# Sparse attention and a two-layer expert on one core: full-array attention matmuls over 64-query tiles, laid between the expert's matmuls by hand

## The chip, the core and the metric

The kernel runs on one core of one Trainium2 chip. A core has a matrix engine (TensorE, PE in the profile), a vector engine (VectorE, DVE), a scalar engine for activations (ScalarE, ACT), a general one (GpSimd, POOL), an engine that issues transfers (SyncE, SP), and 16 DMA engines that move data between HBM and the on-chip memory SBUF. TensorE reads its operands from SBUF and writes to a second on-chip memory, PSUM, from which VectorE and ScalarE read. Both memories have 128 partitions (rows).

The metric is device time in microseconds. The kernel before takes 463.11 us, the median of 3 runs (462.93 to 463.98).

## The reference

The inputs are `q`, `k`, `v` of 4 batches x 8 heads x 768 positions x 64, and the weights `moe_w_in` (512 x 2048) and `moe_w_out` (2048 x 512), all in float32. What matters of the computation:

```python
block, window = (32, 16);  nb = S // block          # 24 blocks of 32 keys
k_sum = k.reshape(B, H, nb, block, D).max(axis=3)   # one key per block: the maximum
v_sum = v.reshape(B, H, nb, block, D).mean(axis=3)  # one value per block: the mean
scores_l = scale * q @ k.T, kept only where |i - j| < window, else -1e9
scores_s = scale * q @ k_sum.T + log(block)
a = softmax(concatenate([scores_l, scores_s], axis=-1))
attn_out = a @ concatenate([v, v_sum])              # B, H, S, D
x = attn_out.transpose(0, 2, 1, 3).reshape(B * S, H * D)   # 3072 x 512
h = x @ w_in
out = (h / (1 + exp(-1.702 * h))) @ w_out           # 3072 x 512
```

A query thus sees at most 31 near keys, each with its own weight, and 24 block keys. Since `log(block)` is added to a block's score, its weight is 32 times `exp`, which with the block's mean is `exp` times the block's sum. The kernels use that: the block's value is the sum of its 32 values and its entry in the denominator is 32.

## The kernel before, in words

The kernel has three stages in a row. The framework places the waits and buffers and decides within each engine in which order instructions go out; it may move one ahead of another that isn't ready.

**Attention** (L121 to L216) is a loop over 4 batches and 8 heads. Per head, q and k come in as six row tiles of 128 positions side by side (`raw`, L124 and L127), ScalarE casts them to bf16 (`cb`, L131), and six TensorE transposes (L134) give q with the head dimension on partitions 0 to 63 and k on 64 to 127. VectorE copies this out of PSUM (`qkT`, L138), and a transfer moves the k half down to partitions 0 to 63 (`kTb`, L141), since both operands of a matmul lie on the same partitions. VectorE takes the maximum over each block of 32 keys (`ksumT`, L144). The values come in as eight windows of 128 keys, one per tile of 96 queries (`vwf`, L151 to L155), and are cast by ScalarE (`vwin`, L158) with a column of ones added, so that the value matmul also makes the denominator. Eight small matmuls against constant 0/1 matrices sum the values by block (`ps_vs`, L170).

Queries go in tiles of 96, four tiles to a group, two groups to a head. One matmul of 384 columns makes a group's scores against the 24 block keys (L179), four of 96 columns its scores against the window's 128 keys (L185). ScalarE exponentiates both (L190, L192), and VectorE multiplies the near part by a 0/1 mask (L194). Each query tile then has two value matmuls into the same output: one over 128 near keys (L200), one over 24 block keys (L203). VectorE divides by the denominator (L208, L210), and a transfer writes the group to a buffer in HBM, `x_bridge` (L213).

**Weights** (L230 to L239): two transfers of 4 MB each and two casts on ScalarE.

**The expert** (L241 to L270) is a loop over six chunks of 512 tokens. Four transposing transfers read `x_bridge` back (`xsb`, L244). Sixteen groups of four matmuls of 512 columns make `ph` (L252), and ScalarE applies the activation (`gT`, L257). Then four groups of sixteen matmuls make `po` (L262), which ScalarE copies out (`osb`, L268) and a transfer stores (L270).

All transfers go out on SP's queue. GpSimd only makes the constants at the start.

## Time and profile before

| | |
|---|---|
| median of 3 runs | 463.11 us (462.93 to 463.98) |
| span of the profiled execution, first to last instruction | 460.9 us |
| TensorE busy in the span | 370.1 us (80%), 2032 matmuls |
| ScalarE busy | 186.0 us (40%) |
| VectorE busy | 111.8 us (24%) |
| GpSimd busy | 6.9 us (1%) |
| bytes moved | 45.46 MB, 124064 of 131771 packets under 512 bytes |
| chain of work that ended last | PE 66%, DMA 14%, DVE 10%, ACT 5% |

The profile comes from one execution, and its span is 2.2 us below the median of the runs. In it a group of instructions is named by its line, engine, operation, output and input; behind the bar stand its busy time, the mean duration of one in ns, and the idle time of the engine before it with what ended that. PEld is TensorE's loading of a matmul's fixed operand, which overlaps its matmuls. Matmuls are pipelined, so the distance between two starts (the pitch) says more than the duration of one. PEclk is the clock granted to TensorE, as a share of full speed.

### The profile page before, as it was taken

Reading aid. Unit: us, or ns where it says so; the run is one execution under the profiler, and the core shown is the slowest. Engines: PE = TensorE matmul, PEld = TensorE weight load, DVE = VectorE, ACT = ScalarE, POOL = GpSimd, SP = SyncE. Lnnn points to the kernel's source line nnn. Section 1 sums busy time; section 2 is a strip of 40 time slices with the busy share of each in tenths; the row PEclk is TensorE's granted clock in tenths of the full one; section 3 lists DMA queues with packets and bytes.
Section 4 is the critical chain, followed back from the end, with each engine's and each line's share of the span. In section 5 each row is a group of like instructions: output and inputs, shape, how many; then the busy total and the mean of one; then the engine's idle time right before and its main releaser. Section 6 shows DMA issues by size and latency. Waiting matters only on the chain.

```text
span 460.9 us, 5530 instructions
## 1 busy us (share of the span) xinstructions
PE 370.1 (80%) x2032; PEld 206.4 (45%) x2048; DVE 111.8 (24%) x320; ACT 186.0 (40%) x316; POOL 6.9 (1%) x38
## 2 busy tenths in 40 slices
PE   3986777876967877777777703799999999999996
PEld 2554455554644544555454500344444444444442
DVE  1443534443444443444444400000000000000000
ACT  3443343433434343342443255643616345262541
POOL 5000000000000000000000000000000000000000
PEclk9999999999999999999999999899999999999999
DMA  7445544544455365364445699222040410101101
GB/s 156 87 100 112 111 97 96 108 102 105 98 120 115 78 139 110 80 133 90 105 106 111 213 387 249 46 36 102 7 109 23 75 64 1 73 18 47 46 24 69
DMA packets 131771, 45.46 MB, mean 99 GB/s; under 512 B 124064, under 2 KB 126112, under 8 KB 131232
## 3 DMA queue, kind: packets, MB, share of 16 engines
q1 hardware_dynamic: 131744, 45.11, 40.3%
q8 instruction: 16, 0.26, 0.2%
q14 instruction: 11, 0.09, 0.1%
HBM read 29.36 MB, written 9.44 MB: 84 GB/s over the span
## 4 chain that ended last, share of the span: by engine, by line
PE 66%; DMA 14%; DVE 10%; ACT 5%; issue 2%; SPq 2%; ACTq 0%
PE ph L252 18%; PE po L262 18%; PE ps_av L203 12%; PE ps_av L200 11%; DMA kTb<-qkT 9%; DVE ksumT L144 6%; PE ptp L134 4%; DMA w_out_f<-in_moe_w_out_dram 4%; PE ps_blk L179 3%; DVE qkT L138 2%; ACT w_out_sb L239 2%; DMA raw<-in_k_dram 1%; ACT cb L131 1%; DVE xg L210 1%; ACT a_loc L190 1%
## 5 line engine op out<-in xcount | busy, mean ns | idle before, releaser
L252 PE MATMUL ph<-xsb,w_in_sb 128*128 128x512 bf16 x377 | 86.9, 388 | 23.4 <-DMA xsb<-x_bridge 18.3
L262 PE MATMUL po<-w_out_sb,gT 128*128 128x512 bf16 x375 | 83.2, 379 | 0.4
L190 ACT ACTIVATE a_loc<-ps_loc 128x384 bf16<-128x384 f32 x64 | 28.1, 488 | 105.8 <-PE ps_loc L185 104.2
L200 PE MATMUL ps_av<-vwin,a_loc 128*96 128x65 bf16 x256 | 70.2, 288 | 0.0
L252 PEld LDWEIGHTS <-w_in_sb 128*128 128x128 bf16 x384 | 38.0, 99 | 71.1 <-issue 27.7
L203 PE MATMUL ps_av<-vsum,a_blk 24*96 24x65 bf16 x256 | 68.2, 283 | 0.7
L257 ACT ACTIVATE gT<-ph 128x512 bf16<-128x512 f32 x96 | 57.2, 597 | 26.6 <-PE ph L252 26.5
L262 PEld LDWEIGHTS <-gT 128*128 128x128 bf16 x384 | 37.6, 98 | 45.3
L185 PE MATMUL ps_loc<-qkT,kTb 64*128 64x96 bf16 x256 | 27.4, 274 | 33.8 <-DMA kTb<-qkT 33.6
L200 PEld LDWEIGHTS <-a_loc 128*96 128x96 bf16 x256 | 38.7, 154 | 32.6 <-DVE a_loc L194 18.9
L203 PEld LDWEIGHTS <-a_blk 24*96 24x96 bf16 x256 | 36.7, 153 | 18.1 <-ACT a_blk L192 3.0
L268 ACT ACTIVATE osb<-po 128x512 f32<-128x512 f32 x24 | 14.3, 597 | 68.8 <-PE po L262 66.0
L185 PEld LDWEIGHTS <-kTb 64*128 64x128 bf16 x256 | 19.2, 131 | 39.5 <-DMA kTb<-qkT 38.0
L144 DVE TENSOR_REDUCE ksumT<-kTb 64x24 bf16<-64x768 bf16 x32 | 30.0, 937 | 26.0 <-DMA kTb<-qkT 26.0
L158 ACT ACTIVATE vwin<-vwf 128x512 bf16<-128x512 f32 x32 | 20.0, 626 | 35.3 <-issue 27.0
L134 PE MATMUL ptp<-ident,cb 128*128 128x128 bf16 x192 | 26.8, 309 | 8.9 <-ACT cb L131 7.8
L208 DVE RECIPROCAL recip<-ps_av 96x4 f32<-96x4 f32 x64 | 11.4, 179 | 83.6 <-PE ps_av L203 83.6
L131 ACT ACTIVATE cb<-raw 128x768 bf16<-128x768 f32 x32 | 26.8, 838 | 11.3 <-DMA raw<-in_k_dram 11.1
L179 PE MATMUL ps_blk<-qkT,ksumT 64*24 64x384 bf16 x64 | 26.1, 507 | 4.5 <-DVE ksumT L144 4.5
L192 ACT ACTIVATE a_blk<-ps_blk 24x384 bf16<-24x384 f32 x64 | 27.2, 470 | 5.8 <-PE ps_blk L179 5.8
L170 PE MATMUL ps_vs<-vwin,P 128*24 128x65 bf16 x64 | 15.0, 235 | 15.1 <-ACT vwin L158 14.8
L210 DVE TENSOR_TENSOR xg<-ps_av,recip 96x256 bf16<-96x256 f32 x64 | 26.0, 415 | 1.4
(36 smaller groups left out, 131.4 us busy)
## 6 DMA issues: line engine op xcount, KB each, us to landing
raw<-in_q_dram SPq DMA_DIRECT2D x32, 192.0 KB, 3.0
raw<-in_k_dram SPq DMA_DIRECT2D x32, 192.0 KB, 3.1
vwf<-in_v_dram SPq DMA_DIRECT2D x32, 192.0 KB, 2.9
out_dram<-osb SPq DMA_DIRECT2D x24, 256.0 KB, 2.0
w_in_f<-in_moe_w_in_dram SPq DMA_DIRECT2D x1, 4096.0 KB, 12.6
w_out_f<-in_moe_w_out_dram SPq DMA_DIRECT2D x1, 4096.0 KB, 16.6
kTb<-qkT SPq DMA_DIRECT2D x32, 96.0 KB, 2.1
x_bridge<-xg SPq DMA_DIRECT2D x64, 48.0 KB, 1.7
```

Source lines behind the costliest of these rows:

```text
L131: nc.scalar.activation(out=cb, in_=raw, func=ACT.Copy)
L134: nc.tensor.matmul(out=ptp[:, j * 128:(j + 1) * 128], lhsT=cb[:, j, :], rhs=ident, is_transpose=True, start=True, stop=True)
L144: nc.vector.tensor_reduce(out=ksumT, in_=kTb.rearrange("d (n s) -> d n s", s=block), axis=AX.X, op=ALU.max)
L179: nc.tensor.matmul(out=ps_blk, lhsT=ksumT, rhs=q_grp, start=True, stop=True)
L185: nc.tensor.matmul(out=ps_loc[:, i * QT:(i + 1) * QT], lhsT=kTb[:, ws:ws + 128], rhs=q_sl, start=True, stop=True)
L190: nc.scalar.activation(out=a_loc, in_=ps_loc, func=ACT.Exp, scale=scale)
L200: nc.tensor.matmul(out=ps_av[:, i, :], lhsT=a_loc[:, sl], rhs=vwin[:, t, :], start=True, stop=False)
L203: nc.tensor.matmul(out=ps_av[:, i, :], lhsT=a_blk[:, sl], rhs=vsum, start=False, stop=True)
L210: nc.vector.tensor_mul(xg, ps_av[:, :, 0:D], recip.to_broadcast([QT, GRP, D]))
L252: nc.tensor.matmul(out=ph, lhsT=w_in_sb[:, ko, nt * 128:(nt + 1) * 128], rhs=xsb[:, ko, :], start=(ko == 0), stop=(ko == KO - 1))
L257: nc.scalar.activation(out=gT[:, nt, :], in_=ph, func=ACT.Gelu_apprx_sigmoid)
L262: nc.tensor.matmul(out=po, lhsT=gT[:, nt, ms * 128:(ms + 1) * 128], rhs=w_out_sb[:, nt, :], start=(nt == 0), stop=(nt == NT - 1))
```

## The change

The attention is written anew, the order of the work is written out by hand, and the way of `x` through HBM is gone.

**Order.** Every engine's instructions behind the constants go through `_Ordered`, which tells the framework to keep them in program order.

**Loads.** All of a batch's q, k and v are loaded together, 24 transfers of 192 KB on SP's queue (`load_batch`), into tiles that hold two heads side by side (`load_qk`) or all eight (`load_v`). The values are loaded once and not as overlapping windows. Batches 0 and 1 are loaded at the start, batch b + 2 within batch b's expert. The casts of the first batch are on VectorE (k), ScalarE (q) and both ScalarE and GpSimd (v); those of the later ones are on GpSimd alone. The weights come in by eight transfers on GpSimd's queue that cast on the way.

**Layout.** Heads go in four pairs, with one head on partitions 0 to 63 and the other on 64 to 127. Queries go in 12 tiles of 64 (`QT`, `NQ`). For each tile, `kx` has 128 columns: its own 64 keys, the 24 block keys, and 32 halo keys, 16 from each neighbour (an odd tile has them in another order); the few columns left are zero or masked. `qz` holds a tile's queries of both heads, with zeros where the partitions belong to the other head, so that one matmul of 128 rows x 128 columns, with 128 columns streamed, makes all scores of a tile for both heads (`scores`). ScalarE exponentiates four tiles at once, and VectorE multiplies by one mask. `vw` holds the values with the same row order per tile: own values, block sums, halo. The block sums are made by six matmuls of 512 columns against a constant `E` (`vsum`), and six transfers within SBUF put them and the halos into `vw`. The value matmul takes two tiles as its fixed operand (128 columns) and streams both tiles' values (130 columns, `values`); of its four quarters, two are used. The result is divided by VectorE into `x_sb`, transposed by TensorE, and copied to `xT`, which stays on chip (`tx`).

**Interleaving.** The expert goes by batch (768 tokens): `ff_in` makes 384 columns at a time, `ff_out` is cut in four parts of four matmuls. During batch b's `ff_in` the transposes and block work of batch b + 1 (`tk`, `tq`, `vsum`) are placed between its groups; behind each of the 24 parts of `ff_out` one piece of batch b + 1's attention is placed. Batch 0's attention stands alone ahead of that.

The core of the diff. All of the old function from `QT = 96` on, shown above, is taken out; the masks and the other constants are left out here.

```diff
+class _Ordered:
+    def __getattr__(self, name):
+        f = getattr(self._eng, name)
+        def call(*a, **kw):
+            r = f(*a, **kw)
+            self._tc.keep_in_program_order(r)
+            return r
+        return call
...
+    keep = ctx.enter_context(tc.tile_pool(name="keep", bufs=1))
+    stage = ctx.enter_context(tc.tile_pool(name="stage", bufs=2))
+    castp = ctx.enter_context(tc.tile_pool(name="cast", bufs=3))
+    attp = ctx.enter_context(tc.tile_pool(name="att", bufs=2))
+    outp = ctx.enter_context(tc.tile_pool(name="outp", bufs=3))
+    psc = ctx.enter_context(tc.tile_pool(name="psc", bufs=3, space=bass.MemoryType.PSUM))
+    pav = ctx.enter_context(tc.tile_pool(name="pav", bufs=1, space=bass.MemoryType.PSUM))
+    pmm = ctx.enter_context(tc.tile_pool(name="pmm", bufs=3, space=bass.MemoryType.PSUM))
...
+    def load_batch(b):
+        for p in range(NP):
+            raw[b, "k", p] = load_qk(b, p, "k")
+            raw[b, "q", p] = load_qk(b, p, "q")
+            if p == 0:
+                raw[b, "v"] = load_v(b)
+    load_batch(0)
...
+    def load_weights():
+        for c in range(4):
+            pool.dma_start(out=w_in_sb[:, :, c * 512:(c + 1) * 512], in_=wi[:, :, c * 512:(c + 1) * 512])
+        for c in range(4):
+            pool.dma_start(out=w_out_sb[:, c * 4:(c + 1) * 4, :], in_=wo[:, c * 4:(c + 1) * 4, :])
...
+    def cast_qk(b, p, which, first):
...
+        if not first:
+            pool.tensor_copy(out=t, in_=src)
+        elif which == "k":
+            dve.tensor_copy(out=t, in_=src)
+        else:
+            act.activation(out=t, in_=src, func=ACT.Copy)
...
+    def cast_v(b, par, first):
+        for j in range(NJ):
+            if first and j % 2 == 0:
+                act.activation(out=dst[:, j], in_=src[:, j], func=ACT.Copy)
+            else:
+                pool.tensor_copy(out=dst[:, j], in_=src[:, j])
+    def vsum():
+        ps = psc.tile([128, H * D], F32, name="ps_vs", tag="sc")
+        for j in range(NJ):
+            o = 20 - 4 * j
+            pe.matmul(out=ps, lhsT=E[:, o:o + 128], rhs=vw5[:, j, 0, :, 0:D],
+                      start=(j == 0), stop=(j == NJ - 1))
+        dve.tensor_copy(out=vs[:, :, 0:D], in_=ps.rearrange("p (h d) -> p h d", d=D))
+        sp.dma_start(out=vw5[64:64 + nb, :, 0], in_=vs[64:64 + nb].unsqueeze(1)
+                     .to_broadcast([nb, NJ, H, VC]))
+        sp.dma_start(out=vw5[0:nb, :, 1], in_=vs[0:nb].unsqueeze(1)
+                     .to_broadcast([nb, NJ, H, VC]))
+        sp.dma_start(out=vw5[96:112, 1:NJ, 0], in_=vw5[112:128, 0:NJ - 1, 1])
...
+    def tk(p):
+        ps = trans(src.rearrange("p j h d -> p j (h d)"))
+        dve.tensor_copy(out=cols(0, [[256, NJ], [192, 2], [1, 64]]), in_=ps.rearrange("p (j e c) -> p j e c", e=2, c=64))
+        dve.tensor_reduce(out=ks, in_=ps.rearrange("p (n s) -> p n s", s=block), axis=AX.X, op=ALU.max)
+        dve.tensor_copy(out=cols(256 + 96, [[256, NJ - 1], [-176, 2], [1, 16]]),
+                        in_=pcols(128 - 16, [[128, NJ - 1], [16, 2], [1, 16]]))
+        dve.tensor_copy(out=cols(128 + 32, [[256, NJ], [-48, 2], [1, 16]]),
+                        in_=pcols(64 - 16, [[128, NJ], [16, 2], [1, 16]]))
+        dve.tensor_copy(out=cols(64, [[256, NJ], [64, 2], [1, nb]]),
+                        in_=ks.unsqueeze(1).unsqueeze(1).to_broadcast([128, NJ, 2, nb]))
+    def tq(p):
+        ps = trans(src.rearrange("p j h d -> p j (h d)"))
+        for hh in range(2):
+            dve.tensor_copy(out=qz[p][r, :, hh, :], in_=ps[r].rearrange("p (t c) -> p t c", c=QT))
+    def scores(p, g):
+        ps = psc.tile([128, 4, 2, QT], F32, name="ps_s", tag="sc")
+        for i in range(4):
+            t = 4 * g + i
+            pe.matmul(out=ps[:, i].rearrange("p h c -> p (h c)"), lhsT=kx[p][:, t, :],
+                      rhs=qz[p][:, t].rearrange("p h c -> p (h c)"), start=True, stop=True)
+        ts = slice(4 * g, 4 * g + 4)
+        act.activation(out=a[:, :, ts, :].rearrange("p h t c -> p t h c"), in_=ps,
+                       func=ACT.Exp, scale=scale)
+        dve.tensor_mul(a[:, :, ts, :], a[:, :, ts, :],
+                       mk[:, ts, :].unsqueeze(1).to_broadcast([128, 2, 4, QT]))
+    def values(p, half):
+        ps = pav.tile([128, 2, 512], F32, name="ps_av", tag="av")
+        for hh in range(2):
+            for jp in range(3):
+                j = half * 3 + jp
+                pe.matmul(out=pv[:, hh, jp, :].rearrange("p (e c) -> p e c", e=2),
+                          lhsT=a[:, hh, 2 * j:2 * j + 2, :].rearrange("p t c -> p (t c)"),
+                          rhs=vw[:, 2 * j:2 * j + 2, 2 * p + hh, 0:D + 1], start=True, stop=True)
+        dve.reciprocal(out=rc, in_=pv.rearrange("p h j (e c) -> p h j e c", e=2)[..., D])
+        for e in range(2):
+            r = slice(e * 64, e * 64 + 64)
+            dve.tensor_mul(xo[r], pv[r, :, :, e * 65:e * 65 + D],
+                           rc[r, :, :, e:e + 1].to_broadcast([64, 2, 3, D]))
+    def tx(p):
+        ps = trans(x_sb.pop(p).rearrange("p j h d -> p j (h d)"))
+        dve.tensor_copy(out=xT[p], in_=ps)
+    def ff_in(nt, half):
+        ph = pmm.tile([128, HALF], F32, name="ph", tag="mm")
+        for ko in range(KO):
+            pe.matmul(out=ph, lhsT=w_in_sb[:, ko, nt * 128:(nt + 1) * 128],
+                      rhs=xT[ko][:, hs], start=(ko == 0), stop=(ko == KO - 1))
+        act.activation(out=gT[:, nt, hs], in_=ph, func=ACT.Gelu_apprx_sigmoid)
+    def ff_out(b, ms, part):
+        for nt in range(4 * part, 4 * part + 4):
+            pe.matmul(out=po, lhsT=gT[:, nt, ms * 128:(ms + 1) * 128],
+                      rhs=w_out_sb[:, nt, :], start=(nt == 0), stop=(nt == NT - 1))
+        if part == 3:
+            act.activation(out=osb, in_=po, func=ACT.Copy)
+            sp.dma_start(out=out[r0:r0 + 128, :], in_=osb)
+    att = [("s", 0, 0), ("s", 0, 1), ("s", 0, 2), ("v", 0, 0),
+           ("s", 1, 0), ("v", 0, 1), ("s", 1, 1), ("s", 1, 2), ("x", 0, 0), ("v", 1, 0),
+           ("s", 2, 0), ("v", 1, 1), ("s", 2, 1), ("s", 2, 2), ("x", 1, 0), ("v", 2, 0),
+           ("s", 3, 0), ("v", 2, 1), ("s", 3, 1), ("s", 3, 2), ("x", 2, 0), ("v", 3, 0),
+           ("v", 3, 1), ("x", 3, 0)]
+    cast_qk(0, 0, "k", True)
+    cast_qk(0, 0, "q", True)
+    tk(0)
+    tq(0)
+    cast_v(0, 0, True)
+    cast_v(0, 1, True)
+    load_weights()
+    load_batch(1)
+    vsum()
+    for p in range(1, NP):
+        cast_qk(0, p, "k", True)
+        cast_qk(0, p, "q", True)
+    done = 1
+    for kind, p, g in att:
+        if kind == "s" and g == 0 and p >= done:
+            tk(p)
+            tq(p)
+            done += 1
+        piece(kind, p, g)
+    for b in range(B):
+        nxt = b + 1 < B
+        if nxt:
+            cast_qk(b + 1, 0, "k", False)
+            cast_qk(b + 1, 0, "q", False)
+            cast_v(b + 1, 0, False)
+            cast_qk(b + 1, 1, "k", False)
+            cast_qk(b + 1, 1, "q", False)
+            cast_v(b + 1, 1, False)
+            todo = [lambda: tk(0), lambda: tq(0), lambda: tk(1), lambda: tq(1), vsum,
+                    lambda: (cast_qk(b + 1, 3, "k", False), tk(2)),
+                    lambda: (cast_qk(b + 1, 3, "q", False), tq(2)),
+                    lambda: tk(3), lambda: tq(3)]
+        for nt in range(NT):
+            for half in range(2):
+                ff_in(nt, half)
+            if nt == 3 and nxt:
+                cast_qk(b + 1, 2, "k", False)
+                cast_qk(b + 1, 2, "q", False)
+            if nt >= 4 and todo:
+                todo.pop(0)()
+            if nt == 6 and b + 2 < B:
+                load_batch(b + 2)
+        pieces = list(att) if nxt else []
+        for ms in range(NJ):
+            for part in range(4):
+                ff_out(b, ms, part)
+                if pieces:
+                    piece(*pieces.pop(0))
```

359 lines of the change are left out of this document (149 added, 210 removed).

## The prediction

> **What bounds the kernel now.** I cut the span at the last attention matmul (264.6 us) and at the first feed-forward matmul of the unbroken run (291.2), and asked for the busy time of each engine in the three stretches (columns: stretch, length, busy and count of each engine, TensorE clock, DMA share, GB/s).
>
> ```profile
> core 0 of [0], span 460.9 us
> ...
> 0.00:264.60 264.60, 201.61 (x1280) 130.82 (x1280) 111.26 (x319) 99.09 (x193) 6.87 (x38) 1.00 0.51 111
> 264.60:291.20 26.60, 3.68 (x7) 1.04 (x9) 0.57 (x2) 15.97 (x5) 0.00 (x0) 0.99 0.90 291
> 291.20:460.90 169.70, 164.80 (x745) 74.57 (x759) 0.00 (x0) 70.90 (x119) 0.00 (x0) 0.99 0.17 49
> ```
>
> Attention takes 264.6 us, a bridge 26.6, the feed-forward stage 169.7. The last is TensorE work end to end. Attention has TensorE busy three quarters of the time, so next come the costliest groups (shapes apart; busy us, mean ns | idle before) and the order of TensorE in one head.
>
> ```profile
> L252 PE MATMUL ph<-xsb,w_in_sb 128*128 128x512 bf16 x377 | 86.9, 388 | 23.4 <-DMA xsb<-x_bridge 18.3 <-ACT gT L257 4.4 <-issue 0.2
> L262 PE MATMUL po<-w_out_sb,gT 128*128 128x512 bf16 x375 | 83.2, 379 | 0.4
> L200 PE MATMUL ps_av<-vwin,a_loc 128*96 128x65 bf16 x256 | 70.2, 288 | 0.0
> L203 PE MATMUL ps_av<-vsum,a_blk 24*96 24x65 bf16 x256 | 68.2, 283 | 0.7
> ...
> L200 PEld LDWEIGHTS <-a_loc 128*96 128x96 bf16 x256 | 38.7, 154 | 32.6 <-DVE a_loc L194 18.9 <-DVE vsum L173 0.3 <-issue 0.3
> L252 PEld LDWEIGHTS <-w_in_sb 128*128 128x128 bf16 x384 | 38.0, 99 | 71.1 <-issue 27.7
> ...
> L185 PE MATMUL ps_loc<-qkT,kTb 64*128 64x96 bf16 x256 | 27.4, 274 | 33.8 <-DMA kTb<-qkT 33.6
> ...
> L134 PE MATMUL ptp<-ident,cb 128*128 128x128 bf16 x192 | 26.8, 309 | 8.9 <-ACT cb L131 7.8 <-DVE vsum L173 0.5
> ...
> L179 PE MATMUL ps_blk<-qkT,ksumT 64*24 64x384 bf16 x64 | 26.1, 507 | 4.5 <-DVE ksumT L144 4.5
> ```
> ```profile
> 101.85 0.82 PE L134 MATMUL ptp<-ident,cb 128*128 128x128 bf16 x6
> ...
> 105.41 0.82 PE L185 MATMUL ps_loc<-qkT,kTb 64*128 64x96 bf16 x8 [2.19 <-DMA kTb<-qkT]
> ...
> 108.35 0.28 PE L203 MATMUL ps_av<-vsum,a_blk 24*96 24x65 bf16 x1
> 108.57 0.29 PE L200 MATMUL ps_av<-vwin,a_loc 128*96 128x65 bf16 x1
> ```
>
> The 512 matmuls of L200 and L203 follow each other at 0.22 us though they stream only 65 columns: more than half of the 201.6 us. Their 96-column weights take 154 ns to load, against 99 ns for 128 columns. And the whole stage is at half pace: a 384-column matmul of L179 lasts 507 ns, a 512-column one of L252 usually 379. The clock column does not say so. At the feed-forward's start it does:
>
> ```profile
> 292.02 0.15 PEld L252 LDWEIGHTS <-w_in_sb 128*128 128x128 bf16 x1 [0.28 <-issue]
> 292.45 0.15 PEld L252 LDWEIGHTS <-w_in_sb 128*128 128x128 bf16 x1 [0.28 <-issue]
> ...
> 294.12 5.93 PEld L252 LDWEIGHTS <-w_in_sb 128*128 128x128 bf16 x28 [0.25 <-issue]
> ```
> ```profile
> 292.00:294.00 2.00, 2.00 (x6) 0.73 (x5) 0.00 (x0) 0.60 (x1) 0.00 (x0) 0.50 0.31 70
> 296.00:298.00 2.00, 2.00 (x11) 0.88 (x9) 0.00 (x0) 1.20 (x3) 0.00 (x0) 1.00 0.00 0
> ```
>
> At clock 0.50 the 512-column pitch is 0.43 us, at 1.00 it is 5.93/27 = 0.22. The transposes' pitch, (0.82 - 0.31)/5 = 0.10 us for 128 columns, is the 0.50 pace (0.43/4), so I read all of attention as run at 0.50, before the first clock record. Dense feed-forward matmuls brought the clock up within 3 us of 291.2.
>
> **The change, part by part.** Before: 264.6 + 26.6 + 165.6 (291.2 to the last matmul's end, 456.8) + 4.1 of tail = 460.9. After, the terms are a head that ends when batch 0's attention is done, TensorE work of four feed-forward batches with the attention of three more laid between, and the same tail.
>
> (1) Feed-forward, all batches. L252's 384 matmuls of 512 columns become 512 of 384, L262 stays at 384. At 0.216 us for 512 columns and 0.162 for 384: 83 + 83 = 166 us. GELU hides under it: 32 per batch at the 488 ns that L190 takes for the same 128x384, 15.6 us against 20.8 of TensorE.
>
> (2) Small matmuls of batches 1 to 3. Per batch 72 transposes (128 columns), 48 scores (128) and 48 values (130), where the old kernel had 320 small ones; all load 128-column weights. 504 in the loop. Bounds: 0.05 us (half of 0.10, if the full clock is all that counts) and 0.10 (no gain from it). L185 pins the loads: eight of 128-column weights at (0.82 - 0.27)/7 = 0.078 at half clock, so a load does not keep a matmul beyond that. I take 0.07: 35 us (25 to 50). The 18 block-mean matmuls of 512 columns add 3.9. The Trainium skill's page "TensorE: Matmul & The Clock Gate", section "Back-to-back issue gap", gives about 81 ns for a sustained 128-column stream of load and matmul; by it, an estimate, this term is 41 us.
>
> (3) What goes: L141's, L213's and L244's transfers, the weight casts on ScalarE, and with them the 26.6 us bridge. Weights are loaded and cast by GpSimd's DMA queue under batch 0. What comes back is a table load at each of seven switches between Exp and GELU:
>
> ```profile
> L131 ACT ACT_TABLE_LOAD x1 | 1.3, 1283 | 4.6 <-DMA raw<-in_k_dram 4.6
> ```
>
> 1.28 us each; three output buffers, each good for a 0.65 us group of TensorE, cover most of it, and without that cover it would be 9 us.
>
> (4) The head. Batch 0's value matmuls need `vw` complete, whose six copies from `vs` go out on SP's queue behind the 24 loads of batch 0 and the 24 of batch 1 (4.72 MB each). Rows for the rate, and for what a small transfer meets behind a big one on that queue:
>
> ```profile
> 2.00:8.00 6.00, 0.98 (x7) 0.65 (x7) 0.33 (x1) 2.76 (x4) 5.50 (x30) 1.00 1.06 227
> 260.00:268.00 8.00, 4.37 (x22) 2.52 (x19) 2.30 (x7) 1.72 (x4) 0.00 (x0) 1.00 1.01 414
> ```
> ```profile
> L213 SPq DMA_DIRECT2D x_bridge<-xg x64: 317/350/872, 16.5 to 265.2; - x64
> ...
> DMA to landing us min/median/max: 1.7/1.7/6.9
> ```
>
> 256-byte rows saturate at 227 GB/s, the weights' long rows at 414. The worst x_bridge write, 6.9 us instead of 1.7, is one issued with a weight load ahead of it. So the copies wait: 9.44/0.227 = 42 us after the start at 2, plus 4 for themselves, 48 us if the weights (8.39 MB at 414 GB/s, 20 us of engine time, issued once GpSimd is through its masks and casts) yield; 68 if they go first. Nothing here shows two queues sharing. I take the middle: values start at 58. TensorE takes its instructions in the written order, so three of four pairs' `tk`, `tq`, scores are queued behind that wait, and `VectorE`'s and `ScalarE`'s work with them.
>
> What follows is VectorE's pace:
>
> ```profile
> L144 DVE TENSOR_REDUCE ksumT<-kTb 64x24 bf16<-64x768 bf16 x32 | 30.0, 937 | 26.0 <-DMA kTb<-qkT 26.0
> L190 ACT ACTIVATE a_loc<-ps_loc 128x384 bf16<-128x384 f32 x64 | 28.1, 488 | 105.8 <-PE ps_loc L185 104.2 <-PE ps_av L200 1.7
> ...
> L210 DVE TENSOR_TENSOR xg<-ps_av,recip 96x256 bf16<-96x256 f32 x64 | 26.0, 415 | 1.4
> L194 DVE TENSOR_TENSOR a_loc<-a_loc,gmask 128x384 bf16<-128x384 bf16 x64 | 22.8, 357 | 4.4
> ...
> L138 DVE COPY qkT<-ptp 128x768 bf16<-128x768 bf16 x32 | 17.8, 556 | 20.7 <-PE ptp L134 19.0
> ...
> L208 DVE RECIPROCAL recip<-ps_av 96x4 f32<-96x4 f32 x64 | 11.4, 179 | 83.6 <-PE ps_av L203 83.6
> ...
> L173 DVE CAST vsum<-ps_vs 24x65 bf16<-24x65 f32 x32 | 6.8, 212 | 16.3 <-PE ps_vs L170 16.3
> ```
>
> A pair: `tk` 0.56 + 0.94 + halos 2 x 0.33 + block keys 0.4 (between L173's 65 and L194's 384 elements) = 2.6; `tq` 1.1; three mask products of 512 at 0.42; two times a reciprocal 0.18 and two products of 384 at 0.55; `tx` 0.56. That is 8.1 us; four pairs less the 4.9 done before the wait leave 27.5, and each pair has about 1.6 us in which VectorE waits for its first scores and exponentials, the end 3 more: 36 us. Head: 94.
>
> (5) In the loop VectorE has 15 us in the 26 of the `ff_in` half and 18 in the 30 of the other, ScalarE 11 in the latter. What shows: the last two values and the last transpose of each batch, with one output tile and one part of 0.86 us between steps of 1.7, about 3 us a batch, 9; and 2 for the clock's rise. The queues cost nothing by this count: batch 3's loads, on SP, come free to issue when batch 0's last store is out, take 21 us of the engines, and `vw`'s copies behind them land some 25 us into `ff_in`, 4 before the first values of batch 2 want them. Were the loads late by more, each us would stop TensorE there. Batch 2's loads go out behind batch 0's copies, before `ff_in` starts, and meet nothing.
>
> (6) GpSimd casts q, k, v of the next batch: 12,288 elements a partition in 20 instructions. Rows for it are only fills and masks:
>
> ```profile
> L64 POOL TENSOR_SCALAR_AFFINE_SELECT gmask<-gmask 128x96 bf16<-128x96 bf16 x8 | 1.9, 268 | 0.0
> ...
> L60 POOL MEMSET gmask<- 128x384 bf16 x2 | 0.8, 420 | 0.0
> ```
>
> From 0.8 ns an element (L60's slope) to twice that with 0.2 us each: 13 to 24 us. `vw`'s part may start once the batch's values are done, and `tk`/`tq` of the third and fourth pair want theirs 16 to 21 us later, so it is nothing at the lower end and about 3 us a batch at the upper; I take nothing, as a fill is the nearest row. Without that cover each late cast holds TensorE's queue, `ff_in` included.
>
> (7) Tail, unchanged:
>
> ```profile
> 451.68 5.13 PE L262 MATMUL po<-w_out_sb,gT 128*128 128x512 bf16 x22
> ...
> 456.89 0.60 ACT L268 ACTIVATE osb<-po 128x512 f32<-128x512 f32 x1 [2.86 <-PE po L262]
> ```
>
> 460.9 - 456.8 = 4.1 us. **Sum:** 94 + 166 + 39 + 11 + 4 = 314; the median of the runs, 463.11, is 2.2 above the profiled span, so 316 us.
>
> **Rivals.** *Head shorter.* The loads win over the weights: values start at 48, all ends at 306. For it: 256-byte rows are many and GpSimd must make the weights' descriptors; against: nothing but long rows.
>
> *Casts late.* GpSimd beyond 2 ns an element makes `tk`/`tq` and `vw` wait, about 8 us a batch: 340.
>
> *The interleave exists only on paper.* TensorE's order is fixed, so a piece whose exponential or product is late stops the feed-forward part behind it. If each of 72 pieces shows 0.7 us of the 1.7 us chain: +50, 366. For it: L200's loads waited 18.9 us for masks before; against: two feed-forward parts, 1.7 us, lie between most producers and users.
>
> *Slower: the clock stays at 0.50 in the loop.* Attention ran so with TensorE 76% busy, and its transposes and short matmuls now sit inside the feed-forward stage. At half clock 205 us of loop work double: 521. It is slower than before once (463 - 316)/205 = 72% of that work runs at half pace. Against: the old feed-forward stage held 1.00. The skill's page named above, Part 1, has the clock fall after an idle window of about 3.4 us and, in Part 4, transposes not counted as busy; by that rule a stretch of 24 transposes and waits could drop it, but no stretch here is free of dense matmuls that long.
>
> **How the numbers follow.** Forecast (306 to 332) 0.52; head shorter 0.15; casts late 0.15; paper interleave 0.14; half clock 0.03; the rest 0.01. With the bounds of the head (-10, +10), the small matmuls (-10, +15) and the casts (+9), and 36 us of batch 0's chain for which no row has the interplay, the range is 292 to 358; it leaves out most of the paper interleave and the half clock. All but the half clock are faster: 0.96; within 0.2% (what a measurement of this kernel can tell from no change) 0.01; slower 0.03.
>
> **What would show it.** The first value matmul at 48 to 68 us, released by a DMA into `vw`; the last transpose of batch 0's output near 94; 512-column pitch 0.22 and small ones 0.05 to 0.08 after it; no GpSimd release above 3 us a batch; TensorE busy above 90% from 100 on. A loop of more than 240 us, or a first value matmul outside those bounds, makes it wrong.

## The result and the profile after

The changed kernel takes **315.81 us** (median of 4 runs, 314.48 to 316.54), the kernel before 463.02 us beside it (462.86 to 463.98). The ratio is **0.681, 95% interval 0.679 to 0.683**. The forecast of 316 us is met, though not by its own terms: four of them were off, and that the errors cancelled so closely is luck. In the tables below, where one of a kernel's four runs lay over 1.5% above its fastest, the ratio leaves that run out, while median and range keep it.

First the page of the changed kernel: 40 slices of the span (a slice is 7.8 us, each digit tenths of busy time), the DMA queue of the weights (packets, MB, share of the 16 engines over the span), and the chain that ended last.

```profile
span 312.4 us, 4176 instructions
...
PE   1230000003565899999989999999999999999995
...
PEclk9985555555555699999999999999999999999999
DMA  9999999999990003111169981010040111100121
...
q0 software_dynamic: 4224, 4.19, 8.0%
...
PE 64%; SPq 21%; DVE 11%; issue 2%; DMA 1%; ACT 0%; ACTq 0%
```

The kernel has two parts. For 13 slices TensorE does little or waits, at half clock; from there it is full, at full clock. In the first part the DMA engines are saturated, and 21% of the chain is SP's queue, against 2% before. The same by stretches (length, then busy time and count of PE, PEld, DVE, ACT and POOL, then clock, DMA share, GB/s):

```profile
40.00:60.00 20.00, 0.00 (x0) 0.00 (x0) 0.78 (x2) 0.31 (x1) 0.00 (x0) 0.50 1.22 214
...
80.00:100.00 20.00, 10.89 (x93) 9.55 (x93) 16.75 (x40) 4.99 (x8) 0.48 (x1) 0.50 0.76 140
103.80:158.80 55.00, 53.71 (x398) 32.31 (x400) 31.42 (x69) 27.55 (x52) 13.10 (x21) 0.98 0.13 37
158.80:212.80 54.00, 52.55 (x398) 31.84 (x400) 31.41 (x69) 28.68 (x53) 13.18 (x21) 1.00 0.61 130
212.80:266.80 54.00, 52.55 (x397) 31.85 (x399) 31.08 (x69) 28.67 (x53) 8.09 (x12) 1.00 0.15 43
266.80:308.80 42.00, 41.73 (x225) 21.84 (x224) 0.56 (x1) 19.90 (x38) 0.00 (x0) 1.00 0.10 38
```

The last four rows are the expert's four batches: 205 us, TensorE busy 97 to 99%. A batch with the next batch's attention in it takes 54.0 us, the last one, without, 42.0. So attention costs 12 us a batch inside the expert, where the old kernel gave it 264.6/4 = 66. What is left to win without taking work off TensorE stands nearly all ahead of 103.8. TensorE in order, there and at the seam between two batches:

```profile
72.19 0.81 PE L27 MATMUL ps_av<-vw,a_sb 128*128 128x130 bf16 x6 [53.59 <-DMA vw<-vw]
...
77.53 0.61 PE L27 MATMUL ps_s<-qz,kx 128*128 128x128 bf16 x4 [3.25 <-DVE qz L27]
...
86.44 0.61 PE L27 MATMUL ps_s<-qz,kx 128*128 128x128 bf16 x4 [3.29 <-DVE qz L27]
...
103.81 7.91 PE L27 MATMUL ph<-xT,w_in_sb 128*128 128x384 bf16 x40
...
111.56 0.50 PE L27 MATMUL ps_t<-ident,kb 128*128 128x128 bf16 x6
111.89 1.46 PE L27 MATMUL ph<-xT,w_in_sb 128*128 128x384 bf16 x8
...
156.58 0.52 PE L27 MATMUL ps_av<-vw,a_sb 128*128 128x130 bf16 x6 [0.62 <-DVE x_sb L27]
...
158.58 0.34 PE L27 MATMUL ps_t<-ident,x_sb 128*128 128x128 bf16 x3 [0.45 <-DVE x_sb L27]
...
159.57 6.17 PE L27 MATMUL ph<-xT,w_in_sb 128*128 128x384 bf16 x37 [0.16 <-DVE xT L27]
```

TensorE stood 53.6 us for the copies into `vw`. Then a pair of batch 0 takes 8.9 us (77.53 to 86.44), 3.3 of which it waits for VectorE's `qz`. Six transposes take 0.33 us in the loop (111.56 to 111.89), 0.055 each. Of the costliest groups, those that the steps below speak of (every instruction goes through one helper, so all have line 27 and are told apart by their tiles):

```profile
L27 PE MATMUL ph<-xT,w_in_sb 128*128 128x384 bf16 x512 | 90.0, 329 | 0.5 <-DVE xT L27 0.5
...
L27 PE MATMUL ps_av<-vw,a_sb 128*128 128x130 bf16 x192 | 19.0, 243 | 57.0 <-DMA vw<-vw 53.6
...
L27 POOL CAST vw<-vf 128x512 bf16<-128x512 f32 x42 | 24.0, 613 | 101.9 <-DMA out_dram<-osb 74.3
...
L27 POOL CAST kb<-kf 128x768 bf16<-128x768 f32 x12 | 9.9, 827 | 55.0 <-PE ps_t L27 54.2
...
L27 ACT ACT_TABLE_LOAD x8 | 10.3, 1283 | 6.8 <-DMA qf<-in_q_dram 6.7
```

The value matmuls, 138 us of the old kernel, are 19. No TensorE group waits for GpSimd (POOL) or for a table load.

### The profile page after: what moved, and what is told of

The parts are those of the page before. It is cut to its first block, busy times and chain, and to the rows that moved or that the text cites. A ratio compares the mean times of both kernels' runs of the same rounds, so it can differ in the third digit from the quotient of the medians.

```text
span 312.4 us, 4176 instructions
## 1 busy us (share of the span) xinstructions
PE 222.7 (71%) x1578; PEld 135.5 (43%) x1592; DVE 130.5 (42%) x306; ACT 121.1 (39%) x218; POOL 59.2 (19%) x126
## 4 chain that ended last, share of the span: by engine, by line
PE 64%; SPq 21%; DVE 11%; issue 2%; DMA 1%; ACT 0%; ACTq 0%
PE ph L27 27%; PE po L27 25%; SPq L27 21%; DVE x_sb L27 5%; PE ps_t L27 4%; PE ps_av L27 4%; PE ps_s L27 3%; PE ps_vs L27 1%; DVE xT L27 1%; DVE kx L27 1%; DVE rc L27 1%; DVE qz L27 1%; DMA vw<-vw 1%; DVE a_sb L27 1%; DVE ks L27 1%
## 5 line engine op out<-in xcount | busy, mean ns | idle before, releaser
L27 PE MATMUL ph<-xT,w_in_sb 128*128 128x384 bf16 x512 | 90.0, 329 | 0.5 <-DVE xT L27 0.5
L27 ACT ACTIVATE gT<-ph 128x384 bf16<-128x384 f32 x128 | 62.9, 491 | 38.1 <-PE ph L27 37.6
L27 PEld LDWEIGHTS <-w_in_sb 128*128 128x128 bf16 x512 | 49.3, 99 | 31.6 <-issue 2.5
L27 PE MATMUL ps_av<-vw,a_sb 128*128 128x130 bf16 x192 | 19.0, 243 | 57.0 <-DMA vw<-vw 53.6
L27 ACT ACTIVATE a_sb<-ps_s 128x512 bf16<-128x512 f32 x48 | 27.7, 595 | 80.8 <-PE ps_s L27 80.7
L27 POOL CAST vw<-vf 128x512 bf16<-128x512 f32 x42 | 24.0, 613 | 101.9 <-DMA out_dram<-osb 74.3
L27 DVE TENSOR_TENSOR a_sb<-a_sb,mk 128x512 bf16<-128x512 bf16 x48 | 20.2, 425 | 45.4 <-ACT a_sb L27 45.0
L27 DVE TENSOR_TENSOR x_sb<-ps_av,rc 64x384 bf16<-64x384 f32 x64 | 35.5, 555 | 1.5
L27 PE MATMUL ps_s<-qz,kx 128*128 128x128 bf16 x192 | 20.1, 238 | 10.0 <-DVE qz L27 9.8
L27 PEld LDWEIGHTS <-kx 128*128 128x128 bf16 x192 | 15.8, 108 | 20.0 <-DVE qz L27 10.6
L27 DVE COPY qz<-ps_t 64x768 bf16<-64x768 bf16 x32 | 17.6, 551 | 0.9 <-PE ps_t L27 0.7
L27 ACT ACT_TABLE_LOAD x8 | 10.3, 1283 | 6.8 <-DMA qf<-in_q_dram 6.7
```

The lines of the kernel that those rows point to most:

```text
L27: r = f(*a, **kw)
```

## Experiments on the head

The theory after the result: the copies into `vw` wait for 9.44 MB of loads ahead of them on SP's queue, and the weights, on GpSimd's queue, slow these loads down. The timeline of SP's queue in the changed kernel (start, length of issuing, what, how many) shows the place:

```profile
17.57 1.72 SPq L27 DMA_DIRECT2D kf<-in_k_dram  x2
...
21.98 10.71 SPq L27 DMA_DIRECT2D kf<-in_k_dram  x2
32.74 9.72 SPq L27 DMA_DIRECT2D qf<-in_q_dram  x2
...
65.17 1.91 SPq L27 DMA_DIRECT2D vw<-vs  x2
```

Batch 0's 24 loads are issued by 22 us at 0.9 us each. The first four of batch 1 take 5 us each, and that is when the weights, issued from 18 to 24 us, are on the way. Three runs take one thing away each, and one takes both. The table behind them gives the first value matmul and the start of the expert, both from the traces.

**Batch 1's loads behind the copies.**

```diff
     load_weights()
-    load_batch(1)
     vsum()
+    load_batch(1)
```

> Changed kernel with the loads of batch 1 issued behind the six copies into vw instead of ahead of them; nothing else. Theory (queue order): the copies wait because SP's queue serves the 24 loads of batch 1 ahead of them, and the weights take 25 us of the engines meanwhile. Behind batch 0's loads alone (which the weights push out to about 38 us) they land near 42, the first value matmul comes 30 us earlier than the 72.2 of the changed kernel, and the whole takes about 286 us. Rival (late next): another chain, batch 1's loads now ending near 70 or the casts on GpSimd, takes the place of the wait; then less than 10 us are gained (306 or more).

**The weights behind the copies.** Two small GpSimd copies read from what the six transfers write, so GpSimd issues the weights only then.

```diff
-    load_weights()
     load_batch(1)
     vsum()
+    gate = consts.tile([128, 2], BF16, name="gate")
+    pool.tensor_copy(out=gate[64:64 + nb, :], in_=vw[64:64 + nb, 0, H - 1, D:VC])
+    pool.tensor_copy(out=gate[32:48, :], in_=vw[32:48, 1, H - 1, D:VC])
+    load_weights()
```

> Changed kernel with the weights issued only once the six copies have landed (two small GpSimd copies that read them stand ahead of the weights on its queue); the copies stay behind both batches' loads. Theory: 9.44 MB at about 200 GB/s is 47 us, so the values start near 52 instead of 72, the weights land by 77, ahead of the expert's start at 84, and the whole takes about 296 us. That would put 20 of the 72 us on the weights. Rival: if the weights had only filled gaps of the loads, the values start after 65 and the whole takes 308 or more.

**Both.** The two edits together: `vsum()`, `load_batch(1)`, the gate, `load_weights()`.

> Changed kernel with both edits: SP's queue has batch 0's loads, the copies, batch 1's loads; the weights go out when the copies have landed. Theory: the values start near 30 us, batch 0's attention takes the same 32 us, the expert starts near 62, and the whole takes about 273 us. Late next: weights and batch 1's loads (48 us of engine time from 30 on) end near 78, while the expert wants its first weights at 62 and batch 1's values by 76; that can give back up to 10 us (283).

**The copies on ScalarE's queue.** The order of loads stays; batch 0's copies go out on another queue.

```diff
-    def vsum():
+    def vsum(sp=sp):
...
-    vsum()
+    vsum(act)
```

> Changed kernel with batch 0's six copies into vw issued from ScalarE's queue instead of SP's; the order of all else is as it was. Theory (queue order): the copies pass both batches' loads, the values start near 28 us, and the whole takes about 270 us, with weights (in by 46) and batch 1's loads (in by 70) still ahead of their users. Rival (engines, not queue): the copies share 16 engines with two full queues and crawl; the values start beyond 45 and the whole takes 290 or more.

| | first value matmul | expert starts | median us (range) | ratio to before, 95% |
|---|---|---|---|---|
| changed kernel | 72.2 | 103.8 | 315.81 (314.48 to 316.54) | 0.681 (0.679 to 0.683) |
| batch 1's loads later | 43.6 | 75.5 | 288.72 (287.16 to 291.09) | 0.625 (0.622 to 0.628) |
| weights later | 44.6 | 76.8 | 287.82 (287.43 to 288.30) | 0.621 (0.620 to 0.622) |
| both later | 26.0 | 58.2 | 274.20 (272.55 to 276.94) | 0.590 (0.588 to 0.593) |
| copies on ScalarE | 43.1 | 75.0 | 284.17 (282.09 to 287.21) | 0.612 (0.607 to 0.616) |

Each row of these four traces that carries the first column, in the table's order (the wait of TensorE in brackets):

```profile
43.59 0.81 PE L27 MATMUL ps_av<-vw,a_sb 128*128 128x130 bf16 x6 [25.02 <-DMA vw<-vw]
```
```profile
44.64 0.81 PE L27 MATMUL ps_av<-vw,a_sb 128*128 128x130 bf16 x6 [28.02 <-DMA vw<-vw]
```
```profile
25.97 0.81 PE L27 MATMUL ps_av<-vw,a_sb 128*128 128x130 bf16 x6 [9.23 <-DMA vw<-vw]
```
```profile
43.06 1.10 PE L27 MATMUL ps_av<-vw,a_sb 128*128 128x130 bf16 x6 [24.35 <-DVE a_sb L27]
```

Either cause alone is worth 28 us of wait (72.2 - 43.6, 72.2 - 44.6), both together 46 (72.2 - 26.0). So whichever goes second is worth 18. The traces show that the two hold the copies back in different ways. With only the weights in the way, the copies are issued from 21 to 30 us as the loads end, but the `vw<-vw` ones land 14 us after their issue, where it is 3 us in the changed kernel: they share the engines with the weights. With only batch 1's loads in the way, they land in 3 us, but the first is issued at 37.6 us instead of 19.0: they stand in line on SP's queue. With the weights out of the way the loads were quicker than expected too (44.6 us against 52, and 287.8 in all against 296). Of the 46 us, 42 show in the time (315.8 - 274.2); batch 1's loads, casts and copies are now late, and TensorE waits once for them inside the loop, 2.65 us for batch 1's `vw`.

The copies on ScalarE's queue missed their 270 us. By the last row above, the value matmuls wait for VectorE's masks and not for the copies, and behind the masks stands another transfer. The chain of waits of that run (start, us, what), and the issuing of the four copies `vw<-vw` on ScalarE's timeline:

```profile
25.57 15.56 DMA qf<-in_q_dram
```
```profile
20.55 16.02 ACTq L27 DMA_DIRECT2D vw<-vw  x4
```

The q load of batch 0's last pair, on the way beside the weights, lands at 41.1. ScalarE's instructions stand in the written order, and that pair's cast is ahead of the first pair's exponentials. But the copies were hardly quicker: the last of them was issued only at 36.0 and landed 6 us later, about 42, one us before the values start. What held its issue is not shown. So the rival of this run, that the copies crawl beside two full queues, is right in kind, though its 45 and 290 us were not reached. Moving the copies to another queue gained 32 us of the 42; the transfers had to be put in another order to gain the rest.

**VectorE's pace after the wait.** `n_tq_act` gives the copies of `qz` (pairs 1 to 3) and of `xT` in the head to ScalarE, which is busy 4.99 us of 20 there.

```diff
-            dve.tensor_copy(out=qz[p][r, :, hh, :],
-                            in_=ps[r].rearrange("p (t c) -> p t c", c=QT))
+            if first:
+                act.activation(out=qz[p][r, :, hh, :],
+                               in_=ps[r].rearrange("p (t c) -> p t c", c=QT), func=ACT.Copy)
...
-        dve.tensor_copy(out=xT[p], in_=ps)
+            act.activation(out=xT[p], in_=ps, func=ACT.Copy)
```

> Changed kernel with batch 0's copies into qz (pairs 1 to 3) and xT on ScalarE, idle there, instead of VectorE. Theory (VectorE's pace): 3 x 1.1 + 4 x 0.56 = 5.5 us less on VectorE, 4 to 5.5 us less in all, about 311 us. Rival (the chain from one engine to the next, or TensorE's clock, paces it): less than 1.5 us, as the same copies stand in the same chain.

Measured: 311.41 us (311.10 to 313.27), ratio 0.672 (0.670 to 0.674). The values start at 72.33 as before and the expert at 99.58, so batch 0's attention takes 27.3 us in place of 31.6. All of the gain in time (4.4 us) is in that stretch. VectorE sets its pace: in the changed kernel it is busy 24.7 of those 31.6 us.

**A faster clock in the head.** Three matmuls of 512 columns, whose result nobody uses, behind each of batch 0's pieces.

```diff
         piece(kind, p, g)
+        pw = pmm.tile([128, 512], F32, name="pw", tag="mm")
+        for i in range(3):
+            pe.matmul(out=pw, lhsT=E[:, 20:148], rhs=mk.rearrange("p t c -> p (t c)")[:, 0:512],
+                      start=(i == 0), stop=(i == 2))
```

> Changed kernel with three matmuls of 512 columns on constants, whose result isn't used, behind each of batch 0's 24 pieces. Theory (VectorE paces batch 0's attention): if the clock rises, its small matmuls take half, 168 x 0.05 = 8 us less TensorE time, and the whole stays within 3 us of 316. Rival (the half clock paces it): 5 to 8 us less. If the clock doesn't rise, the 72 matmuls cost 31 us of TensorE time at half clock, more than the gaps hold, and the whole is 10 to 20 us longer; that says nothing of either.

Measured: 323.93 us (322.08 to 324.92), ratio 0.698 (0.695 to 0.701), 8 us more than the changed kernel. The page's clock line and one row of TensorE's timeline:

```profile
PEclk9995555555778799999999999999999999999999
```
```profile
91.51 0.61 PE L27 MATMUL ps_s<-qz,kx 128*128 128x128 bf16 x4 [3.22 <-DVE qz L27]
```

The clock rose only in part. Behind each wait for `qz` it is low again: four score matmuls last 0.61 us there (row above), and 0.39 later in that pair. That wait is as long as it was (3.22 us), though the transposes ahead of it now run at full clock. The dense matmuls stretched a pair to 11 or 12 us from 8.9. So this run doesn't say what the half clock costs in the head; it says that the wait for VectorE is about the same at either clock.

## Experiments on the loop

**The pieces not laid between `ff_out`'s parts** but behind all of them. The same instructions, in another order.

```diff
                 ff_out(b, ms, part)
-                if pieces:
-                    piece(*pieces.pop(0))
+        while pieces:
+            piece(*pieces.pop(0))
```

> Changed kernel with the 24 attention pieces of batches 1 to 3 placed behind the whole of the batch's ff_out instead of between its parts; the transposes and block keys stay within ff_in, the matmuls are the same. Theory (the interleave hides VectorE's chain): alone, a batch's pieces go at VectorE's pace, 4 x (three masks 0.42, two times 0.23 and 1.12, one copy 0.56) = 18 us and some 5 of waits, instead of the 7 us of TensorE time and 2 of waits that they take now: +14 us a batch, +42 in all, about 358 us. Rival (the gain is in the matmuls, not in their place): less than +10 us.

Measured: 367.08 us (366.54 to 367.62), ratio 0.791 (0.789 to 0.794): 51 us more than the change, 9 more than expected. The page's slices, and the stretch of one batch's pieces:

```profile
PE   0400000055579999856899996759999956599996
PEclk9965555555559999965899999557999985589999
```
```profile
152.80:175.80 23.00, 13.01 (x121) 10.76 (x120) 16.98 (x39) 9.79 (x15) 3.56 (x7) 0.69 1.05 208
```

The pieces, which need about 7 us of TensorE when they are laid between dense matmuls (120 at 0.055), take 23.0 by themselves, at VectorE's pace. That is what was expected, 18 and 5. But the clock falls too: the three dips are the three batches. Behind the pieces the first `ph` matmuls run slow until it is up again, 40 in 7.8 us, 40 in 8.5 and 92 in 17.6, where 0.162 each as in the changed kernel gives 6.5, 6.5 and 14.9. These are some 6 us, most of the 9 that were not expected. So dense matmuls laid between the short ones also keep the clock up.

## Experiments on the kernel before

The prediction read two things from the old trace that it could not show: that 96-column fixed operands space the value matmuls at 0.22 us, and that the old attention ran at half clock under a clock column that read 1.00.

**128 columns.** The weights `a_loc` and `a_blk` are 32 columns wider, zeros at the end, and each value matmul takes 128 columns from its query tile's start; only the first 96 rows of the result are used.

```diff
-                    a_loc = app.tile([128, GQ], BF16, name="a_loc", tag="a_loc")
-                    a_blk = app.tile([nb, GQ], BF16, name="a_blk", tag="a_blk")
+                    a_loc = app.tile([128, GQ + 32], BF16, name="a_loc", tag="a_loc")
+                    a_blk = app.tile([nb, GQ + 32], BF16, name="a_blk", tag="a_blk")
...
-                        sl = slice(i * QT, (i + 1) * QT)
+                        sl = slice(i * QT, i * QT + 128)
```

> The kernel before with 128 instead of 96 columns in the fixed operand of both value matmuls (L200, L203); the 32 more are the neighbour tile's or zeros, and their output rows are not used. Reading of the prediction (the 96-column weight load spaces these matmuls): the pitch falls from 0.216 us to 0.10 to 0.12, TensorE loses 50 to 60 us of work in the attention stage, and most of it shows: 405 to 425 us. Rival (the load is not what spaces them): the pitch stays and the whole stays within 3 us of 463.

**128 rows too.** On top of that, the block weights and block values get zero rows up to 128.

```diff
-                vsum = qkp.tile([nb, D + 1], BF16, name="vsum", tag="vsum")
-                nc.vector.tensor_copy(out=vsum, in_=ps_vs)
+                vsum = qkp.tile([128, D + 1], BF16, name="vsum", tag="vsum")
+                nc.gpsimd.memset(vsum, 0.0)
+                nc.vector.tensor_copy(out=vsum[0:nb, :], in_=ps_vs)
...
-                    a_blk = app.tile([nb, GQ + 32], BF16, name="a_blk", tag="a_blk")
+                    a_blk = app.tile([128, GQ + 32], BF16, name="a_blk", tag="a_blk")
```

> b_128cols (the kernel before with fixed operands of 128 columns in its value matmuls) and beside it the block weights and block values padded with zero rows to 128, so that both value matmuls of a pair have a fixed operand of 128 x 128; the zero rows add nothing to the sums. Theory (a fixed operand of 24 rows beside one of 128 keeps the load from running beside the matmul): the distance from matmul to matmul falls from 0.167 to about 0.10 us, some 35 us of TensorE time less, 405 to 425 us in all. Rival (the load just isn't hidden behind so short a matmul, whatever its rows): the distance stays at 0.167 us and the time near 443.

| | distance of two value matmuls | load, ns | median us (range) | ratio to before, 95% |
|---|---|---|---|---|
| before (96 columns, 128 and 24 rows) | 0.216 | 154 | 463 | 1 |
| 128 columns, 128 and 24 rows | 0.167 | 105 | 443.45 (442.48 to 443.99) | 0.956 (0.954 to 0.958) |
| 128 columns, 128 rows | 0.055 | 126 | 412.98 (411.46 to 414.27) | 0.891 (0.888 to 0.894) |

The two groups of loads and three value matmuls of TensorE's timeline in the run with 128 columns, and then three of the one with 128 rows too:

```profile
L202 PEld LDWEIGHTS <-a_loc 128*128 128x128 bf16 x256 | 26.3, 105 | 34.5 <-DVE a_loc L196 19.1 <-DVE vsum L173 0.3 <-issue 0.3
...
L205 PEld LDWEIGHTS <-a_blk 24*128 24x128 bf16 x256 | 23.8, 101 | 18.9 <-ACT a_blk L194 4.9 <-ACT a_loc L192 0.2
```
```profile
102.53 0.24 PE L202 MATMUL ps_av<-vwin,a_loc 128*128 128x65 bf16 x1
102.70 0.23 PE L205 MATMUL ps_av<-vsum,a_blk 24*128 24x65 bf16 x1
102.86 0.24 PE L202 MATMUL ps_av<-vwin,a_loc 128*128 128x65 bf16 x1
```
```profile
107.23 0.24 PE L206 MATMUL ps_av<-vsum,a_blk 128*128 128x65 bf16 x1
107.28 0.24 PE L203 MATMUL ps_av<-vwin,a_loc 128*128 128x65 bf16 x1
107.33 0.24 PE L206 MATMUL ps_av<-vsum,a_blk 128*128 128x65 bf16 x1
```

The distances now add up. Streaming 65 columns at half clock takes 0.055 us, the last row. With operands of 128 and 24 rows in turn, the load stands outside: 0.105 + 0.055 = 0.16, and with 96 columns 0.154 + 0.055 = 0.21. So 128 columns quicken the load, which alone brought 20 us and missed its 405 to 425; equal rows let it run beside the matmul, which brought 30 more and the 405 to 425 that were expected there, with a distance of 0.055 where 0.10 was expected. Whether 96 columns with equal rows would also hide the load wasn't tried. That it is the equal rows and not the full 128 x 128, another matmul of the same kernel suggests: the block sums' fixed operands (L170) have 128 rows but 24 columns, and they follow each other at about 0.056 us ((0.52 - 0.24)/5), as this row of the run with 128 columns has it:

```profile
103.23 0.52 PE L170 MATMUL ps_vs<-vwin,P1ext 128*24 128x65 bf16 x6
```

The Trainium skill says on the page "TensorE: Matmul & The Clock Gate", section "Weight-path perf modes — Fast Weight Load (FWL) and DoubleRow", that a faster load is on when there are 128 weights; the 154 and 105 ns agree. Its section "LDWEIGHTS (loading the stationary operand)" has the load go by columns and not by rows: the 24-row and the 128-row operand agree with 101 and 105 ns, but L170's operands of 24 columns take 110 to 121 ns, so here fewer columns were not quicker.

**Dense matmuls in the old attention**, eight of 512 columns ahead of each group's division, result unused, in a single run.

```diff
+                    pw = psg.tile([128, 512], F32, name="pw", tag="ps_blk")
+                    for i in range(8):
+                        nc.tensor.matmul(out=pw, lhsT=ident, rhs=vwin.rearrange("p t c -> p (t c)")[:, 0:512],
+                                         start=(i == 0), stop=(i == 7))
```

> The kernel before with eight 512-column matmuls on data at hand, result unused, behind each group's value matmuls (512 in all). Reading of the prediction (attention ran at half clock because its TensorE work is thin): with dense work inside, the granted clock goes to 1.00 by its record and the transposes' pitch from 0.10 to 0.05; the 512 matmuls cost 110 us, the old ones lose up to 100 of 201, and the whole is 450 to 510 us. Rival (the old shapes themselves are slow): the pitch of the old matmuls stays, and 110 us come on top (570); if the clock stays low it is 220 on top (680), which leaves the reading open.

Measured: 524.04 us, which matches none of the times expected; the durations decide. The clock line of the page, and the old scores and values at two places:

```profile
PEclk9975879799996967969896697959999999999999
```
```profile
102.73 0.49 PE L179 MATMUL ps_blk<-qkT,ksumT 64*24 64x384 bf16 x1
...
105.44 0.23 PE L200 MATMUL ps_av<-vwin,a_loc 128*96 128x65 bf16 x1
105.60 0.23 PE L203 MATMUL ps_av<-vsum,a_blk 24*96 24x65 bf16 x1
...
106.94 0.33 PE L179 MATMUL ps_blk<-qkT,ksumT 64*24 64x384 bf16 x1
```

Once the clock moves, the column shows it, and the old instructions come in two durations: L179's 384 columns in 0.49 us and in 0.33, the value matmuls 0.216 and 0.157 us apart. The old kernel's are the long ones (L179 507 ns). The reading of half clock held.

## Two versions that put it together

**First.** Both transfers late as above, the output weights later still (when batch 0's expert begins), each pair's `tk` and `tq` one pair ahead, and the head's `qz` and `xT` copies on ScalarE.

```diff
-        if kind == "s" and g == 0 and p >= done:
-            tk(p)
-            tq(p)
-            done += 1
-        piece(kind, p, g)
+        if kind == "s" and g == 2 and p + 1 < NP:
+            tk(p + 1)
+            tq(p + 1, True)
...
             cast_qk(b + 1, 0, "q", False)
+            if b == 0:
+                load_weights(1)
             cast_v(b + 1, 0, False)
```

> Everything that the runs so far point to: SP's queue has batch 0's loads, the copies, batch 1's loads; w_in goes out when the copies have landed and w_out behind GpSimd's casts of batch 1's first pair; batch 0's tk and tq go one pair ahead, with qz and xT copied by ScalarE. Theory: values start at 26 as in the run with both edits, batch 0's attention takes about 26 us instead of 32, the expert starts near 53, and the loop's 205 us grow by 3 to 8 for batch 1's late casts: about 267 us. Rival (batch 1's loads decide): transfers of 26 + 25 + 24 us end at 75 whatever is ahead of them, and batch 1's work gets later by what the head gets shorter: 272 or more.

Measured: 275.12 us (274.56 to 275.76), ratio 0.593 (0.592 to 0.595), no better than both transfers late alone; the 267 us expected were missed. The expert does start at 49.8 us, 8 earlier. But TensorE then waits in the loop, in its timeline:

```profile
64.09 0.51 PE L27 MATMUL ps_t<-ident,kb 128*128 128x128 bf16 x6 [2.15 <-POOL kb L27]
...
92.48 0.81 PE L27 MATMUL ps_av<-vw,a_sb 128*128 128x130 bf16 x6 [7.41 <-DMA vw<-vw]
```

Batch 1's copies into `vw` are late in the same way as batch 0's were: batch 2's loads are ahead of them on SP's queue.

**Second.** Batch 2's loads go behind batch 1's copies, and the output weights behind batch 1's first value cast.

```diff
+            cast_v(b + 1, 0, False)
             if b == 0:
                 load_weights(1)
-            cast_v(b + 1, 0, False)
...
-            if nt == 6 and b + 2 < B:
+            if nt == 9 and b + 2 < B:
```

> z_best with two things put later: the output weights are issued on GpSimd's queue behind batch 1's first value cast, and batch 2's loads are issued behind batch 1's value copies on SyncE's queue. Theory (the 7.4 us wait for batch 1's copies and the 2.2 us wait for the GpSimd cast in z_best come from the order of two queues): both waits go, the expert still starts near 50 us, and the time comes to some 262 to 266 us. Rival (the transfer itself, about 12 MB through the same 16 DMA engines in the first 80 us, decides): the waits move to another transfer and the time stays at 272 or more.

Measured: **261.88 us** (260.33 to 263.03), ratio **0.565 (0.563 to 0.567)**, better than both kernels and than every other run. From its stretches (columns as above):

```profile
25.00:49.00 24.00, 14.91 (x132) 13.11 (x133) 19.20 (x46) 11.40 (x17) 6.37 (x10) 0.99 1.14 211
49.07:103.00 53.93, 53.31 (x393) 31.86 (x392) 29.00 (x67) 28.91 (x52) 16.05 (x25) 0.97 0.92 194
```

Both waits are gone, with the DMA engines 92% busy in batch 0's expert: the order on the queues decided, not the amount moved. What is left ahead of the expert is 25 us until batch 0's values are there, and 24 at VectorE's pace.

## Why the prediction was right in the time and wrong in four terms

| term | predicted | measured | difference |
|---|---|---|---|
| first value matmul | 58 | 72.2 | +14 |
| batch 0's attention from there | 36 | 31.6 | -4 |
| loop: expert and small matmuls | 166 + 39 | 4 x 42.0 + 3 x 10.5 = 199.5 | -5.5 |
| loop: seams and clock | 11 | 205 - 199.5 = 5.5 | -5.5 |
| tail | 4.1 | 3.6 | -0.5 |
| span | 314 | 312.4 | -2 |

The 10.5 of the third row is a batch's 168 short matmuls at 0.055 (9.2) and its six `ps_vs` at 0.216 (1.3).

**What bounds the old kernel: right.** Two things carry it. Half clock was shown by the dense matmuls, and the spacing of the value matmuls by the two shapes. "Their 96-column weights take 154 ns to load" was only part of the cause: 20 us of 50. The other 30 lay in the unlike row counts, of which the prediction says nothing. It did no harm to the sum, since the new matmuls have 128 rows and 128 columns throughout.

**(1) Expert: right.** 42.0 us for the last batch against 166/4 = 41.5; the 512 shorter matmuls and the extra groups show no wait for GELU.

**(2) Small matmuls: right in kind, term too large.** 0.07 was taken between 0.05 and 0.10, with a doubt whether the load holds a matmul back. It doesn't: 0.055 is what streaming alone takes, 7 us less over 504. In the Trainium skill the two figures of the page "TensorE: Matmul & The Clock Gate" part here: section "Wait — 56ns, not 53.3ns?" has 55.6 ns for 128 columns, as the trace has it; "Back-to-back issue gap", quoted in the prediction, has 81 with loads, and by it the loop would have been 13 us longer (504 x 0.026).

**(3) What goes: right.** No bridge, and eight table loads of 1283 ns with no TensorE wait behind them.

**(4) The head: the wrong step is "I take the middle".** The bounds were 48 if the weights yield and 68 if they go first. With the weights out of the way the values started at 44.6, and with them at 72.2, past the upper bound: the weights cost 27.6 us, where the upper bound had 20 and the middle 10. Queue q0's row shows most of it: it holds the 16 engines for 8.0% of 312.4 = 25 us, for 8.39 MB read, or 336 GB/s with the cast on the way, where the prediction took 414 from plain transfers. The prediction named its own test, a first value matmul between 48 and 68, and this failed: by its own words it was wrong here, and the time was met because the terms behind it came out shorter by about as much. The second half, batch 0's attention at VectorE's pace, is right as a mechanism, as the move of copies to ScalarE showed; the period is 8.9 us a pair where 8.1 + 1.6 was taken. (The forecast's sum for this stretch, 27.5 + 4 x 1.6 + 3, is 36.9 and not 36, which changes nothing.)

**(5) Seams: right in kind, half the size.** What shows at the seam are the waits that it named, 0.62 + 0.45 + 0.16 us of waiting in the rows from 156.58 on, and some 1.5 us a batch in all where 3 were taken; the clock's rise cost 1 (55.0 against 54.0).

**(6) Casts: right.** 613 ns for 512 elements and 827 for 768, 13 us a batch, the lower end of 13 to 24, and no wait of TensorE for GpSimd.

**The rivals.** The short head fell with the weights. Late casts fell with (6). The interleave on paper fell: TensorE's waits in the loop are some 1.5 us a batch. That the kernel without the interleave takes 367, against the rival's 366, is chance: the rival priced late pieces between the expert's parts, and the run has all pieces behind them, with a falling clock besides. Half clock in the loop fell: 0.98 and 1.00 in the four stretches.

**Where the 147 us came from.** The shape of the value matmuls alone is worth 50 (463 to 413), the interleave 51 (367 to 316), the bridge was 26.6 us of the old span. These were measured in different kernels and needn't add up; the some 19 that remain would be the other short matmuls, now at full clock, and the transfers of attention that went, and that is argued and not shown. Against it stands the head, 104 us without the expert, of which the second version took 54 away.

## What to carry to other kernels

A short transfer that the next stage needs is as late as everything ahead of it on its queue and everything that shares the engines, so write out the queues' order first: here two transfers put later were worth 42 us. Keep the fixed operands of neighbouring matmuls in one shape, 128 x 128, even with rows of zeros, and lay thin work between dense matmuls, which hides its chain and holds the clock. And when a forecast hits, compare its terms one by one: this one was the sum of +14 and three smaller errors the other way.

## What the runs showed of the hardware that was not expected

- Loads of fixed operands with 128 rows and 24 rows in turn don't run beside the matmuls: 0.167 us apart, against 0.055 once both have 128 rows. Equal rows with 24 columns throughout (L170) run at about 0.056.
- The clock column reads full until the first clock record, and whether a record comes early differs between executions. The changed kernel's executions of 315.37 and 316.54 us have a mean clock of 0.863 and 0.999. The run with the copies on ScalarE reads 1.00 throughout while its value matmuls last up to 315 ns in the head against 219 in the loop; the durations are the better clock.
- While 2 KB rows with a cast on the way ran on GpSimd's queue, SP's issues of loads with 256-byte rows took 5 us each in place of 0.9.
- The clock fell within a single batch's attention of 23 us with TensorE busy 13.0 of them (mean 0.69).
- GpSimd's cast from float32 to bf16 takes 613 ns for 512 elements a partition and 827 for 768.
